# First loads of a fused attention and GEGLU block interleaved, a weight load cut by columns, and two of the first row norms moved to ScalarE

## The chip, the cores and the metric

The kernel runs on one core of one Trainium2 chip. The time is device time in microseconds (us) of one execution. TensorE is the matmul engine (PE in the profile), VectorE is DVE, ScalarE is ACT, GpSimd is POOL, SyncE is SP.

## The reference, cut to what matters

A transformer block with adaptive layer norm: linear attention, then a GEGLU feed-forward network. There are 2048 rows of 1024 columns in bf16, and the hidden width of the network is 3584.

```python
mod = (_silu(c) @ w_mod).reshape(c.shape[0], 6, 1, -1)
sa, ca, ga, sb, cb, gb = ...                        # six modulation rows of 1024
h = _layernorm(x, axis=-1) * (1 + ca) + sa
x = x + ga * _A_ref(h, A_wqkv, A_wo)                # linear attention
h = _layernorm(x, axis=-1) * (1 + cb) + sb
x = x + gb * (_gelu(h @ w_gate) * (h @ w_up) @ w_down)
```

At the start, the first products (V = h W_v) need the normed rows, the scale row `ca` and W_v; soon after, the shift row `sa` is needed.

Of the kernel before, what the change touches and what calls it, by code (L numbers as in the profile page):

```python
# [14 lines left out]
ALU = mybir.AluOpType  # L15
# [281 lines left out]
def kernel(  # L297
# [14 lines left out]
    P = 128  # L312
# [4 lines left out]
    S, D = x_in.shape  # L317
    F = B_w_gate.shape[1]
    KD = D // P
# [3 lines left out]
    TT = TG // P  # L323
# [38 lines left out]
    class Ring:  # L362


        def __init__(self, off, shape, dt, n):
            sz = 4 if dt == FP32 else 2
            for d in shape:
                sz *= d
            sz = max(sz, Plan.LINE)
            self.slots = [view(off + i * sz / KB, shape, dt) for i in range(n)]  # L370
            self.i = 0
# [188 lines left out]
    def load_w(dst, col, n=D, k0=0, k1=KD):  # L560
        sy.dma_start(out=dst, in_=A_wqkv[k0 * P:k1 * P, col:col + n].rearrange("(kd p) n -> p kd n", p=P))
# [41 lines left out]
    class ModRow:  # L603


        def __init__(self, m, wm, before={}):
            self.wm, self.ps, self.loads = wm, None, []
            for i in range(0, KD, 2):
                sy.dma_start(out=wm[:, i:i + 2, :],
                             in_=w_mod[i * P:(i + 2) * P, m * D:(m + 1) * D].rearrange("(k p) n -> p k n", p=P))  # L610
                self.loads.append(plan.ops[-1])
                if i in before:
                    plan.aim(before[i])

        def step(self, i):
            if i == 0:
# [39 lines left out]
        ac.activation(out=rstd, in_=rstd, func=AF.Exp, scale=-0.5)  # L656
        return rstd

    def ln_rows(xt):
        mv = ln_stats(xt)  # L660
        rstd = act_rstd(mv)
        xh = xh_ring()
        ve.tensor_scalar(out=xh, in0=xt, scalar1=mv[:, 0:1], scalar2=rstd[:, 0:1],
                                op0=ALU.subtract, op1=ALU.mult)
        return xh

    def keep_warm(n, cols):

        for _ in range(n):
            te.matmul(psD()[:, 0:cols], lhsT=ident, rhs=selb.rearrange("p a b -> p (a b)")[:, 0:cols],  # L670
                             start=True, stop=True, skip_group_check=True)
# [7 lines left out]
        ve.tensor_copy(out=hs0[:, 0:KH, tl * P:(tl + 1) * P], in_=src[0])  # L679
        ac.activation(out=hs0[:, KH:KD, tl * P:(tl + 1) * P], in_=src[1], func=AF.Copy)  # L680

    def scale_wv(n):
        for kd in range(KD):
            ve.tensor_scalar_mul(out=Wvs[:, kd, n * NW:(n + 1) * NW], in0=Wv[:, kd, n * NW:(n + 1) * NW],
                                 scalar1=opcA[:, kd:kd + 1])

    def v_plain(tl, n):

        ps = psV0()
        for k in range(KD):  # L690
            te.matmul(ps, lhsT=hs0[:, k, tl * P:(tl + 1) * P], rhs=Wvs[:, k, n * NW:(n + 1) * NW],
                      start=(k == 0), stop=(k == KD - 1), skip_group_check=True)
        ac.activation(out=vta[:, tl][:, 4 * n:4 * n + 4, 0:P], in_=ps.rearrange("p (g e) -> p g e", e=P), func=AF.Copy)

    def start_phase():

        xs, loads = [], []
        for tt in range(TT):
            xs.append(load_x(tt))
            loads.append(plan.ops[-1])  # L700
            if tt == 0:
                plan.aim(c_load)
        ca = ModRow(1, wm_ca, {0: loads[0], 2: loads[1], 4: loads[2], 6: loads[3]})
        load_w(Wv[:, 0:KH, 0:NW], 2 * D, NW, 0, KH)
        load_w(Wv[:, KH:KD, 0:NW], 2 * D, NW, KH, KD)
        load_w(Wv[:, :, NW:D], 2 * D + NW, NW)
        plan.chain.append(plan.ops[-1])
        sa = ModRow(0, wm_sa)
        plan.chain += sa.loads
        load_w(Wk[:, :, 0:NW], D, NW)  # L710
        ve.tensor_copy(out=identb[0:KD, :], in_=ident[0:KD, 0:KD])
        pcc = psM(BF16)[:, 0:KD]
        te.transpose(pcc, c8[0:KD, :], identb[0:KD, :])
        ve.tensor_copy(out=ccol, in_=pcc)
        ac.activation(out=esig, in_=ccol, func=AF.Exp, scale=-1.0)
        ve.tensor_scalar_add(out=esig, in0=esig, scalar1=1.0)
        ve.reciprocal(out=esig, in_=esig)
        tt_op(scol, ccol, esig, ALU.mult)
        ve.tensor_copy(out=srep, in_=scol[:, :, None].to_broadcast((P, KD, DH)))
        c_done = plan.ops[-1]  # L720
        halves = [[psT(F16).rearrange("p (k t) -> p k t", k=4) for _ in range(2)] for _ in range(2)]
        xh, done = [], []
        for i, x in enumerate(xs):
            n = len(plan.ops)
            xh.append(ln_rows(x))
            if i > 1:
                plan.pairs += [(done[i - 2], op) for op in plan.ops[n:] if op.eng == "DVE"]
            done.append(plan.ops[-1])
            if len(xh) == 1:
                plan.aim(c_done)  # L730
        for i in range(KH):
            if i < 3:
                start_tile(halves[i % 2], i, xh[i])
            if i == 0:
                keep_warm(1, NW)
            ca.step(i)
        ca.columns(opcA, 1.0, lambda: keep_warm(2, NW))
        scale_wv(0)
        for tl in range(TT):
            v_plain(tl, 0)  # L740
            if tl == 1:
                start_tile(halves[1], 3, xh[3])
        scale_wv(1)
        v_plain(0, 1)
        v_plain(1, 1)
        for i in range(KH):
            sa.step(i)
        sa.columns(modT[:, 0:KD], 0.0, lambda: v_plain(2, 1))
        v_plain(3, 1)
        for kd in range(KD):  # L750
            ve.tensor_scalar(out=hr1[0][:, kd, :], in0=hs0[:, kd, :], scalar1=opcA[:, kd:kd + 1],
                             scalar2=modT[:, kd:kd + 1], op0=ALU.mult, op1=ALU.add)
        return plan.ops[-1]
# [18 lines left out]
    def ln1_block(b):  # L772
        plan.ahead = 4000 if b > 1 else 14000
        for tl in range(TT):
            xt = load_x(b * TT + tl)
            if b == 1:
                plan.chain.insert((1, 2, 5, 7)[tl], plan.ops[-1])
            mv = ln_stats(xt)
            rstd = pool_rstd(mv)
            nb = nb_ring()  # L780
            gp.tensor_scalar(out=nb, in0=mv[:, 0:1], scalar1=rstd, scalar2=-1.0, op0=ALU.mult, op1=ALU.mult)
            xh = xh_ring()
            ac.activation(out=xh, in_=xt, func=AF.Identity, scale=rstd, bias=nb)
            gp.dma_start(out=xa_scr[b][tl * P:(tl + 1) * P, :], in_=xh)
        sy.dma_start_transpose(out=hr1[b], in_=xa_scr[b][:])
        if b == NG - 1:
            wd_moves(hr1[b][:, 0, 0:1], NPR)
        for kd in range(KD):
            ve.tensor_scalar(out=hr1[b][:, kd, :], in0=hr1[b][:, kd, :], scalar1=opcA[:, kd:kd + 1],  # L789
                             scalar2=modT[:, kd:kd + 1], op0=ALU.mult, op1=ALU.add)  # L790
        if b != 2:
            paced_moves(hr1[b][:, KD - 1, 0:1], sums_copy[0:1] if b == 1 else sums_add[0:1])
        plan.ahead = 14000
# [1026 lines left out]
```

## The kernel before: the parts that the change and the argument touch

The kernel computes its large products by a fast scheme of block sums and differences (the `A1x = A21 - A22` below are such differences), which is why VectorE has so much to do in it.

**A list scheduler orders the whole program.** The kernel's lines do not issue instructions. They record operations, and at the end a planner orders them. TensorE keeps the recorded order. For VectorE, ScalarE, GpSimd and SyncE the order comes out of 32 forward sweeps over a cost model; each is followed by a backward sweep that gives every operation a new due time, and the best forward sweep is kept.

```python
    def order(self):
        ...
        for op in self.ops:
            op.due = op.n
        for i in range(2 * self.ROUNDS):
            forward(i >= self.ROUNDS)        # sweep over the cost model; the best result is kept
            ...
            t = self.sweep(True, lambda o: (-o.due, -o.n))
            for op in self.ops:
                op.due = best[0] * (1 - op.done / max(t, best[0]))
                if old:
                    op.due += self.KEEP * (old[op.n] - op.due)
            for a, b in [*zip(self.chain, self.chain[1:]), *self.pairs]:
                b.due = max(a.due, b.due)
        return [self.ops[n] for _, n in best[1]]

    def issue(self):
        with self.tc.manual_schedule():
            for op in self.order():
                ...                           # issue op on its engine
```

`plan.chain` is a list of loads that are to be issued in its order.

**The start.** The order of the first loads is set by `aim` and `chain`; the row norms take their statistics on VectorE.

```python
    def ln_rows(xt):
        mv = ln_stats(xt)                     # 2 bn_stats and 1 bn_aggr on VectorE
        rstd = act_rstd(mv)                   # 2 small ScalarE operations
        xh = xh_ring()
        ve.tensor_scalar(out=xh, in0=xt, scalar1=mv[:, 0:1], scalar2=rstd[:, 0:1],
                                op0=ALU.subtract, op1=ALU.mult)
        return xh
    ...
        ca = ModRow(1, wm_ca, {0: loads[0], 2: loads[1], 4: loads[2], 6: loads[3]})
        load_w(Wv[:, 0:KH, 0:NW], 2 * D, NW, 0, KH)
        load_w(Wv[:, KH:KD, 0:NW], 2 * D, NW, KH, KD)
        load_w(Wv[:, :, NW:D], 2 * D + NW, NW)
        plan.chain.append(plan.ops[-1])
        sa = ModRow(0, wm_sa)
        plan.chain += sa.loads
```

## Time and profile before

| kernel before | |
|---|---|
| median of 3 runs | 749.21 us (748.36 to 750.71) |
| median of all 6 runs, those beside the changed kernel included | 748.91 us (747.80 to 750.71) |
| span of the profiled execution | 746.4 us |
| TensorE idle in it | 16.4 us, of which 9.7 before 28.5 us |
| waits of TensorE from 31 to 740 us | 2.2 us, in three groups of 1.2 (four waits, the longest 0.4), 0.5 and 0.5 |

A row of a timeline has the start in us, the length in us, the engine, the line of the kernel, the operation, output and input, and how many such operations the row holds. In square brackets stands how long the engine had been idle before it, and what ended that. `mem` is on-chip memory, `psum` the accumulators, and the names with `_dram` are inputs; `xhs` is the DRAM scratch that the late norm's stores write, and `ts` the one with the sums of w_down.

### The profile page before, as it was taken

Reading aid. Unit: us, or ns where it says so; the run is one execution under the profiler, and the core shown is the slowest. Engines: PE = TensorE matmul, PEld = TensorE weight load, DVE = VectorE, ACT = ScalarE, POOL = GpSimd, SP = SyncE. Lnnn points to the kernel's source line nnn. Section 1 sums busy time; section 2 is a strip of 40 time slices with the busy share of each in tenths; the row PEclk is TensorE's granted clock in tenths of the full one; section 3 lists DMA queues with packets and bytes.
Section 4 is the critical chain, followed back from the end, with each engine's and each line's share of the span. In section 5 each row is a group of like instructions: output and inputs, shape, how many; then the busy total and the mean of one; then the engine's idle time right before and its main releaser. Section 6 shows DMA issues by size and latency. Waiting matters only on the chain.

```text
span 746.4 us, 11439 instructions
## 1 busy us (share of the span) xinstructions
PE 730.0 (98%) x4164; PEld 388.7 (52%) x4164; DVE 589.5 (79%) x1258; ACT 433.0 (58%) x757; POOL 95.8 (13%) x164
## 2 busy tenths in 40 slices
PE   5999999999999999999999999999999999999997
PEld 2444445444444455545454586545555555548664
DVE  6897997577786878777997888678888888888763
ACT  3665576669752768997876234027777777731000
POOL 2331245000001113342311000010000000000000
PEclk9999999999999999999999999999999999999999
DMA  8974479828899979899659799654131322399822
GB/s 298 322 212 132 152 182 163 299 101 258 245 290 257 364 253 261 259 318 227 187 191 237 210 281 314 206 183 132 60 114 57 112 73 98 110 276 302 278 104 71
DMA packets 151832, 152.79 MB, mean 205 GB/s; under 512 B 33824, under 2 KB 128544, under 8 KB 150496
## 3 DMA queue, kind: packets, MB, share of 16 engines
q1 hardware_dynamic: 128832, 122.44, 53.7%
q0 software_dynamic: 20592, 27.53, 15.6%
q10 hardware_dynamic: 2352, 2.10, 0.8%
q8 instruction: 32, 0.52, 0.3%
q14 instruction: 24, 0.20, 0.1%
HBM read 123.34 MB, written 36.04 MB: 214 GB/s over the span
## 4 chain that ended last, share of the span: by engine, by line
PE 84%; DVE 6%; ACT 5%; DMA 3%; issue 1%; SPq 1%; ACTq 0%; DVEq 0%
PE psum L1382 30%; PE psum L1588 13%; PE psum L1632 9%; PE psum L870 8%; PE psum L1393 7%; PE psum L1262 7%; PE psum L940 5%; DVE mem L564 5%; PE psum L969 4%; DMA mem<-in_A_wqkv_dram 2%; DMA mem<-in_w_mod_dram 1%; PE psum L984 1%; ACT mem L815 1%; DVE psum L564 1%; ACT psum L1436 1%
## 5 line engine op out<-in xcount | busy, mean ns | idle before, releaser
L564 DVE TENSOR_TENSOR mem<-mem 128x512 f16<-128x512 f16 (+8 forms) x669 | 307.8, 507 | 23.1 <-ACT mem L815 10.1
L1382 PE MATMUL psum<-mem 128*128 128x512 f16 x1248 | 299.1, 379 | 0.8 <-ACT psum L1436 0.5
L815 ACT ACTIVATE mem<-psum 128x256 f32<-128x256 f32 (+3 forms) x284 | 154.3, 562 | 119.9 <-PE psum L1382 45.1
L564 DVE TENSOR_TENSOR mem<-psum,mem 128x512 f16<-128x512 f32 (+4 forms) x204 | 155.4, 767 | 72.8 <-ACT mem L815 29.5
L1382 PEld LDWEIGHTS <-mem 128*128 128x128 f16 (+1 forms) x1248 | 122.0, 98 | 112.1 <-issue 2.7
L1588 PE MATMUL psum<-mem 128*128 128x512 f16 (+2 forms) x462 | 99.2, 373 | 0.5 <-DVE mem L564 0.5
L1393 PE MATMUL psum<-mem 128*128 128x256 f16 x560 | 89.5, 272 | 1.3 <-DVE psum L564 1.2
L1393 PEld LDWEIGHTS <-mem 128*128 128x128 f16 (+1 forms) x560 | 54.7, 98 | 46.8 <-issue 5.1
L1588 PEld LDWEIGHTS <-mem 128*128 128x128 f16 x462 | 45.2, 98 | 49.8 <-issue 0.7
L1632 PE MATMUL psum<-mem 128*128 128x256 f16 (+1 forms) x588 | 66.2, 273 | 0.0
L870 PE MATMUL psum<-mem 128*128 128x512 f16 (+1 forms) x280 | 62.9, 379 | 0.0
L1632 PEld LDWEIGHTS <-mem 128*128 128x128 f16 x588 | 57.5, 98 | 9.2
L1436 ACT ACTIVATE psum<-psum 128x512 f32<-128x512 f32 x56 | 32.8, 587 | 41.3 <-PE psum L1382 28.9
L1262 PE MATMUL psum<-mem 128*128 128x512 f16 x256 | 56.0, 379 | 0.0
L940 PE MATMUL psum<-mem 128*128 128x512 f16 x224 | 51.2, 379 | 0.0
L564 DVE TENSOR_TENSOR psum<-psum,mem 128x256 f32<-128x256 f32 x80 | 34.3, 429 | 17.7 <-ACT mem L815 17.3
L870 PEld LDWEIGHTS <-mem 128*128 128x128 f16 x280 | 26.9, 97 | 31.8 <-DVE mem L789 1.2
L1262 PEld LDWEIGHTS <-mem 128*128 128x128 bf16 x256 | 24.8, 98 | 30.3 <-issue 0.8
L1453 ACT ACTIVATE mem<-psum 128x512 f16<-128x512 f32 x56 | 33.1, 595 | 10.9 <-PE psum L1382 10.5
L1463 ACT ACTIVATE mem<-mem 128x512 f16<-128x512 f16 x56 | 34.9, 625 | 1.5 <-DVE mem L564 1.1
L940 PEld LDWEIGHTS <-mem 128*128 128x128 f16 (+1 forms) x224 | 21.5, 98 | 27.0 <-issue 2.0
L1049 POOL DMA_DIRECT2D ts<-in_B_w_down_dram x28 | 28.3, 1199 | 9.2 <-DMA ts<-in_B_w_down_dram 8.9
(132 smaller groups left out, 525.3 us busy)
## 6 DMA issues: line engine op xcount, KB each, us to landing
mem<-in_B_w_gate_dram SPq DMA_DIRECT2D x14, 1024.0 KB, 7.0
mem<-in_B_w_up_dram SPq DMA_DIRECT2D x14, 1024.0 KB, 5.4
mem<-in_w_mod_dram SPq DMA_DIRECT2D x24, 512.0 KB, 5.9
mem<-ts SPq DMA_DIRECT2D x6, 1792.0 KB, 6.8
mem<-in_A_x_dram SPq DMA_DIRECT2D x32, 256.0 KB, 7.7
ts<-in_B_w_down_dram POOLq DMA_DIRECT2D x28, 256.0 KB, 6.3
mem<-ub SPq DMA_DIRECT2D x16, 448.0 KB, 6.7
mem<-in_B_w_down_dram SPq DMA_DIRECT2D x12, 448.0 KB, 7.8
```

The costliest lines, as they stand in the source:

```text
L564: ve.tensor_tensor(out=out, in0=a, in1=b, op=op)
L815: ac.activation(out=t, in_=ps, func=AF.Copy)
L870: te.matmul(ps, lhsT=A[:, k, i * P:(i + 1) * P], rhs=B[:, k, :], start=(start and k == 0), stop=(k == KH - 1), skip_group_check=True)
L940: te.matmul(o, lhsT=W[:, k, (j0 + i) * P:(j0 + i + 1) * P], rhs=h_form(a, k), start=(start and k == 0), stop=(k == KH - 1), skip_group_che ...
L1262: te.matmul(psw[:, half, :], lhsT=pqT[b][:, g, tl * P:(tl + 1) * P], rhs=Wp[:, g, half * NW:(half + 1) * NW], start=(g == 0), stop=(g == K ...
L1382: te.matmul(ps, lhsT=a[:, k, e, :], rhs=b[:, k, :], start=(start and k == 0), stop=(k == KH - 1), skip_group_check=True)
L1393: te.matmul(ps, lhsT=self.x[a][:, k, :], rhs=self.y[y][:, k, :], start=(start and k == 0), stop=(k == KH // 2 - 1), skip_group_check=True)
L1436: ac.activation(out=z, in_=x, func=AF.Copy)
L1453: ac.activation(out=o, in_=ps, func=AF.Gelu_apprx_tanh)
L1463: ac.activation(out=o, in_=o, func=AF.Gelu_apprx_tanh)
L1588: te.matmul(psm[:, q, c], lhsT=A[:, i, q * P:(q + 1) * P], rhs=wt[:, i, c], start=(start and i == 0), stop=(i == NPR - 1), skip_group_chec ...
L1632: te.matmul(ps[:, q, :], lhsT=a[:, k, q * P:(q + 1) * P], rhs=y[:, k, :], start=(start and q == 0 and k == 0), stop=(k == NPR // 2 - 1), s ...
```

## The change

The intent is to start TensorE's real work sooner. The scale row's quarters are loaded between the first row tiles, so that it is complete earlier. The first half of W_v comes as two quarters by columns, so that its first 256 columns can be scaled and multiplied before the rest is there. The statistics of row tiles 2 and 3 go from VectorE to ScalarE. The recorded order of the start follows. The diff, cut to its core:

```diff
-    def ln_rows(xt):
+    def ln_rows(xt, by_act):
+        xh = xh_ring()
+        if by_act:
+            nmean, rstd = act_stats(xt)
+            ve.tensor_scalar(out=xh, in0=xt, scalar1=nmean, scalar2=rstd[:, 0:1], op0=ALU.add, op1=ALU.mult)
+            return xh
         mv = ln_stats(xt)
...
-    def scale_wv(n):
+    def scale_wv(c):
         for kd in range(KD):
-            ve.tensor_scalar_mul(out=Wvs[:, kd, n * NW:(n + 1) * NW], in0=Wv[:, kd, n * NW:(n + 1) * NW],
-                                 scalar1=opcA[:, kd:kd + 1])
+            ve.tensor_scalar_mul(out=Wvs[:, kd, c], in0=Wv[:, kd, c], scalar1=opcA[:, kd:kd + 1])
...
+    START_LOADS = "c a0 x0 a1 x1 a2 a3 v0 x2 v1 x3 v2".split()
...
-        ca = ModRow(1, wm_ca, {0: loads[0], 2: loads[1], 4: loads[2], 6: loads[3]})
-        load_w(Wv[:, 0:KH, 0:NW], 2 * D, NW, 0, KH)
-        load_w(Wv[:, KH:KD, 0:NW], 2 * D, NW, KH, KD)
-        load_w(Wv[:, :, NW:D], 2 * D + NW, NW)
-        plan.chain.append(plan.ops[-1])
+        ca = ModRow(1, wm_ca)
+        loads.update((f"a{i}", op) for i, op in enumerate(ca.loads))
+        for name, c in (("v0", slice(0, HB)), ("v1", slice(HB, NW)), ("v2", slice(NW, D))):
+            load_w(Wv[:, :, c], 2 * D + c.start, c.stop - c.start)
+            loads[name] = plan.ops[-1]
+        plan.chain += [loads[name] for name in START_LOADS]
...
-            xh.append(ln_rows(x))
+            xh.append(ln_rows(x, i in (2,3,)))
...
-        scale_wv(0)
-        for tl in range(TT):
-            v_plain(tl, 0)
-            if tl == 1:
-                start_tile(halves[1], 3, xh[3])
-        scale_wv(1)
+        scale_wv(slice(0, HB))
+        for tl in range(2):
+            v_plain(tl, 0, slice(0, HB))
+        scale_wv(slice(HB, NW))
+        start_tile(halves[0], 2, xh[2])
+        for tl in range(2):
+            v_plain(tl, 0, slice(HB, NW))
+        v_plain(2, 0)
+        start_tile(halves[1], 3, xh[3])
+        v_plain(3, 0)
+        scale_wv(slice(NW, D))
```

More of the change, by code (lines that the diff above doesn't have):

```diff
@@ L603, with __init__ @@
     class ModRow:
-        def __init__(self, m, wm, before={}):
+        def __init__(self, m, wm):
             self.wm, self.ps, self.loads = wm, None, []
@@ L611, in __init__ @@
                 self.loads.append(plan.ops[-1])
-                if i in before:
-                    plan.aim(before[i])
         def step(self, i):
@@ L657, in act_rstd @@
         return rstd
-    def ln_rows(xt):
+    def ln_rows(xt, by_act):
[4 more added lines that the diff above has]
+            return xh
         mv = ln_stats(xt)
         rstd = act_rstd(mv)
-        xh = xh_ring()
         ve.tensor_scalar(out=xh, in0=xt, scalar1=mv[:, 0:1], scalar2=rstd[:, 0:1],
@@ L680, in start_tile, with v_plain, v_out @@
         ac.activation(out=hs0[:, KH:KD, tl * P:(tl + 1) * P], in_=src[1], func=AF.Copy)
-    def scale_wv(n):
+    def scale_wv(c):
         for kd in range(KD):
-            ve.tensor_scalar_mul(out=Wvs[:, kd, n * NW:(n + 1) * NW], in0=Wv[:, kd, n * NW:(n + 1) * NW],
-                                 scalar1=opcA[:, kd:kd + 1])
-    def v_plain(tl, n):
-        ps = psV0()
-        for k in range(KD):
-            te.matmul(ps, lhsT=hs0[:, k, tl * P:(tl + 1) * P], rhs=Wvs[:, k, n * NW:(n + 1) * NW],
-                      start=(k == 0), stop=(k == KD - 1), skip_group_check=True)
+            ve.tensor_scalar_mul(out=Wvs[:, kd, c], in0=Wv[:, kd, c], scalar1=opcA[:, kd:kd + 1])
+    v_banks = {}
+    def v_plain(tl, n, c=slice(0, NW)):
+        if c.start == 0:
+            v_banks[tl, n] = psV0()
+        ps = v_banks[tl, n]
+        for k in range(KD):
+            te.matmul(ps[:, c], lhsT=hs0[:, k, tl * P:(tl + 1) * P], rhs=Wvs[:, k, n * NW + c.start:n * NW + c.stop],
+                      start=(k == 0 and c.start == 0), stop=(k == KD - 1), skip_group_check=True)
+        if c.stop == NW:
+            v_out(tl, n, ps)
+    def v_out(tl, n, ps):
         ac.activation(out=vta[:, tl][:, 4 * n:4 * n + 4, 0:P], in_=ps.rearrange("p (g e) -> p g e", e=P), func=AF.Copy)
+    START_LOADS = "c a0 x0 a1 x1 a2 a3 v0 x2 v1 x3 v2".split()
     def start_phase():
-        xs, loads = [], []
+        xs, loads = [], {"c": c_load}
         for tt in range(TT):
             xs.append(load_x(tt))
-            loads.append(plan.ops[-1])
-            if tt == 0:
-                plan.aim(c_load)
-        ca = ModRow(1, wm_ca, {0: loads[0], 2: loads[1], 4: loads[2], 6: loads[3]})
-        load_w(Wv[:, 0:KH, 0:NW], 2 * D, NW, 0, KH)
-        load_w(Wv[:, KH:KD, 0:NW], 2 * D, NW, KH, KD)
-        load_w(Wv[:, :, NW:D], 2 * D + NW, NW)
-        plan.chain.append(plan.ops[-1])
+            loads[f"x{tt}"] = plan.ops[-1]
+        ca = ModRow(1, wm_ca)
[4 more added lines that the diff above has]
+        plan.chain += [loads[name] for name in START_LOADS]
         sa = ModRow(0, wm_sa)
@@ L730, in start_phase @@
                 plan.aim(c_done)
-        for i in range(KH):
-            if i < 3:
-                start_tile(halves[i % 2], i, xh[i])
-            if i == 0:
-                keep_warm(1, NW)
+        keep_warm(1, NW)
+        ca.step(0)
+        start_tile(halves[0], 0, xh[0])
+        for i in range(1, KH):
             ca.step(i)
+        start_tile(halves[1], 1, xh[1])
         ca.columns(opcA, 1.0, lambda: keep_warm(2, NW))
-        scale_wv(0)
-        for tl in range(TT):
-            v_plain(tl, 0)
-            if tl == 1:
-                start_tile(halves[1], 3, xh[3])
-        scale_wv(1)
+        scale_wv(slice(0, HB))
[9 more added lines that the diff above has]
+        scale_wv(slice(NW, D))
         v_plain(0, 1)
@@ L776, in ln1_block @@
             if b == 1:
-                plan.chain.insert((1, 2, 5, 7)[tl], plan.ops[-1])
+                plan.chain.insert(len(START_LOADS) + (0, 1, 4, 6)[tl], plan.ops[-1])
             mv = ln_stats(xt)
```

## The prediction

> **What bounds the kernel now.** I read the page first, then a table of engine busy time by stretch, then the chain of work that ended last over the first 60 us, then TensorE's and SyncE's rows in time order there, then the DMA view for three stretches. The page's first block:
>
> ```profile
> span 746.4 us, 11439 instructions
> PE 730.0 (98%) x4164; PEld 388.7 (52%) x4164; DVE 589.5 (79%) x1258; ACT 433.0 (58%) x757; POOL 95.8 (13%) x164
> ```
>
> TensorE is busy 98%: the whole program holds 16.4 us in which it is not. The change touches the first 30 us only, so what it could ever win is what lies idle there. By stretch (columns: stretch, length, busy us of PE, PEld, DVE, ACT, POOL with counts, granted clock, DMA share, GB/s):
>
> ```profile
> 0.00:8.00 8.00, 0.30 (x3) 0.23 (x4) 5.40 (x28) 2.49 (x6) 3.79 (x22) 1.00 0.68 208
> 8.00:15.00 7.00, 5.88 (x47) 3.02 (x47) 5.48 (x15) 2.56 (x7) 0.00 (x0) 1.00 1.05 370
> 15.00:28.50 13.50, 12.61 (x73) 5.56 (x73) 9.85 (x28) 6.50 (x10) 3.49 (x10) 1.00 1.07 371
> 28.50:40.00 11.50, 11.50 (x69) 5.00 (x69) 10.24 (x25) 7.04 (x11) 3.51 (x7) 1.00 0.78 244
> ```
>
> TensorE idles 7.7 us before 8 us, 1.1 us to 15, 0.9 us to 28.5, and nothing after. The DMA share is 1.05 and more from 8 to 28.5: the queue is full. So before 28.5 us the loads, not TensorE, set the pace. The chain that ended last says which load (start us, us, what):
>
> ```profile
> 7.39 11.51 DMA mem<-in_A_wqkv_dram
> 18.90 0.02 issue
> 18.92 9.11 DMA mem<-in_w_mod_dram
> 28.02 0.04 issue
> 28.07 0.40 PE psum L636 x4
> 28.46 1.83 PE psum L691 x8
> ```
>
> Line 636 is the product of the modulation row. The load issued at 18.92 is the last quarter of the shift row (sa), which lands at 28.02; TensorE takes it at 28.07 and is never idle for long again. TensorE's own rows say the same:
>
> ```profile
> 7.88 1.03 PE L676 MATMUL psum<-mem 128*128 128x128 f16 x8 [5.53 <-DVE mem L663]
> 15.03 4.18 PE L691 MATMUL psum<-mem 128*128 128x512 f16 x16 [0.66 <-DVE mem L684]
> 26.50 0.83 PE L636 MATMUL psum<-mem 128*32 128x512 bf16 x12
> 28.07 0.40 PE L636 MATMUL psum<-mem 128*32 128x512 bf16 x4 [0.73 <-DMA mem<-in_w_mod_dram]
> ```
>
> The reader should see that TensorE reached the shift row at 26.50, did three quarters of it, and waited for the fourth. Anything gained earlier than this ends in that wait, as long as the order there is kept.
>
> **What the Trainium skill says.** "DMA: Bandwidth & Descriptors", section Specifications, gives at least 512 B as the transfer for line rate. The trace disagrees with reading that as "512 B is as good as 2 KB". In three stretches with a full queue, first with rows of 1 KB (W_v), then 2 KB (x and w_mod), then 512 B (quarters of the down weights):
>
> ```profile
> 13.00:17.50 4.50, 3.45 (x19) 1.19 (x19) 3.50 (x11) 0.39 (x3) 0.00 (x0) 1.00 1.10 349
> 20.00:25.00 5.00, 5.00 (x25) 2.28 (x24) 5.00 (x14) 1.65 (x4) 1.41 (x5) 1.00 1.05 387
> 683.00:687.00 4.00, 4.00 (x39) 3.59 (x37) 3.93 (x8) 0.60 (x1) 0.00 (x0) 1.00 1.18 290
> ```
>
> 349, 387 and 290 GB/s. The measurement decides: shorter rows are slower here.
>
> The same page, "Anatomy of one DMA", puts the fixed part of a DMA at about 2.0 us, mostly the wait until the last byte is confirmed. The trace agrees roughly: the first x tile is issued at 1.22 and VectorE's first statistics start at 3.89, 2.67 us, of which 0.262 MB at 387 GB/s is 0.68.
>
> "ScalarE: Activation LUTs", Rules for kernel authors, gives about 0.3 us per ACTIVATE plus 0.83 ns per element, 1.15 us for 1024. The trace has 1.23 us for such a pass (line 783, 128x1024). I use 1.23. "TensorE: Matmul & The Clock Gate", Part 1, says the array runs at half rate until some 3.4 us of sustained work. The trace agrees in kind: eight transposes took 1.03 us at 7.88 and 0.61 us at 19.05.
>
> **The change part by part.**
>
> Order of loads. Before: c, four x tiles (1.05 MB), four quarters of the scale row ca (2.10), W_v in 0.52, 0.52 and 1.05. After: c, x0, ca0, x1, ca1 to ca3, x2, two W_v column quarters (0.52 each), x3, the W_v half (1.05). What follows is unchanged: x4, x5, sa0, sa1, x6, sa2, x7, sa3, then W_k. The bytes ahead of sa3's end are the same 8.39 MB. The order as built confirms this. So in bytes nothing moves at the point that binds.
>
> Row length. The two W_v loads were 512 columns of half the rows (1 KB runs) and are now 256 columns of all rows (512 B runs). 1.05 MB at 349 GB/s is 3.00 us, at 290 it is 3.62. So +0.6 us in the queue, on the path: sa3 lands that much later.
>
> Ramp. The DMA rate is 208 GB/s over the first 8 us; a table by half microseconds has a share of 0.48 and 148 GB/s from 4.5 to 5.0, with four small x loads at the head of the queue. Putting a 0.5 MB load second may keep the engines fuller. I estimate the loss of this dip, against a full queue, at about 1 us, and that the new order recovers a third of it: -0.3 us. This is a guess about a cause that I have not seen.
>
> Norm on ScalarE. For tiles 2 and 3 VectorE loses four statistics of 677 ns and two aggregates of 201 ns, 3.1 us. ScalarE gains two passes of 1.23 us for each, 4.9 us in all, between about 12 and 19 us, where it was busy less than half of the time. x2 now lands near 12.2 us, so its norm is ready near 15.2; x3 near 16.3, ready near 19.2. Off the binding path if TensorE still reaches sa3 in time.
>
> Scaling W_v. Eight operations of 512 columns in 2.43 us (0.30 each) become 16 of 256; from 0.30 at 512 and 0.53 at 1024 columns I estimate 0.2 each, so 3.2 us: +0.8 us of VectorE. It pays for itself by starting after one quarter.
>
> TensorE. 16 products of 512 columns become 32 of 256, equal in columns. My walk, load by load: x0 lands at 3.9, ca0 near 6, x1 near 7. VectorE as built does x1's statistics before it normalises x0, so the first transposes come near 9.0, against 7.88. ca3 lands near 11.6 against 12.9, so the scale columns are ready near 13.7 against 14.6. The first W_v quarter lands near 13.9; products start near 14.2 against 15.0 and are paced by VectorE until about 18; tile 2 ends near 20.8; the half of W_v lands near 19.4 and tile 3's norm waits with it, so tile 3 ends near 23.8; two more groups of eight at 0.217 us bring TensorE to the shift row at 27.2, against 26.50, and through three quarters of it at 28.1. Then sa3: 28.0 + 0.6 - 0.3 = 28.3. The two nearly meet. TensorE passes this point near 28.4 against 28.07.
>
> After it: the same 718.3 us of TensorE work (746.4 - 28.07). The built order of TensorE is the same from there; VectorE and ScalarE have some dozens of neighbours swapped, worth 0.3 us either way by the 2.7 us of waits TensorE has in the rest. Sum: +0.3 us on the span. On 749.2 that is 749.5; I take 0.2 off because such an order is likely to have been kept for a gain. Predicted 749.3 us.
>
> **The rivals.**
>
> 1. The start really shortens. For: the scale row is complete 1.3 us sooner and products start 0.8 us sooner. Against: TensorE's order around sa3 is unchanged and bytes before it are the same. If the ramp recovers its whole 1 us, sa3 lands at 28.0 + 0.6 - 1.0 = 27.6; TensorE, at 28.1, then binds: no change. If it also runs ahead of my walk: -0.7, 748.5 us.
>
> 2. TensorE becomes late. For: tile 3 hangs on a chain x3, four ScalarE steps, VectorE, transposes, two copies, in a queue behind scalings; and its sparser early work may leave the array at half rate longer (transposes and fills cost some 0.9 us more). Against: 32 paced products give it time to speed up. It would pass sa3 near 29.2: +1.1, 750.3 us.
>
> 3. The quarters' short rows cost more, as the slowest of 16 DMA queues decides a landing (sa3's bytes were through by about 26 by the sum of the rates, it landed at 28.0): +1.2, 750.4 us.
>
> **Range and chances.** Before itself ran from 748.36 to 750.71, so a median of few runs moves by some 0.6. The rivals span -0.7 to +1.2. Together: 747.8 to 750.9 for 8 in 10. 2% is 15 us, as much as all idle time of TensorE; faster or slower by that has 1% each, within 2% has 98%.
>
> **What would show it.** Right: the chain of waits again runs through the modulation load into line 634 (the same product), at 28.0 to 28.9 us; TensorE waits there for DMA or arrives with it; DMA near 290 GB/s while the W_v quarters load. Wrong: sa3 landing before 27.5 us (ramp), or TensorE arriving after it with waits on VectorE or ScalarE in front of tile 3 (rival 2), or a difference that arises after 30 us, where I expect none over 0.5.

## More of the kernel before

In the middle of the program, gate and up products of the first half of the rows end, and the down product begins.

**The middle.** Three parts of the program meet near 390 to 405 us. First, the norm of late row tiles writes each normed tile to DRAM; GpSimd issues the store:

```python
        def tile_norm(tl):                    # in late_norm
            xt, xh = x2e_ring(), xhe_ring()
            ...
            ac.activation(out=xh, in_=xt, func=AF.Identity, scale=rstd, bias=nb)
            gp.dma_start(out=xh_scr[g][b % 2][r:r + P, :], in_=xh)      # "the store", L1226
```

Second, GpSimd also issues the moves that make sums of blocks of w_down, from DRAM to DRAM, 256 KB each, half of them accumulating:

```python
    def move(dst, src, add):                  # "the moves", L1049
        gp.dma_start(out=dst, in_=src, **(dict(accum_op=ALU.add) if add else {}))
```

Third, before the down product VectorE makes the differences of blocks of the hidden layer, in chunks:

```python
        for c in range(NPR // NC):            # in down_out
            cs = slice(c * NC, (c + 1) * NC)
            ve.tensor_tensor(out=A1x[:, cs, :], in0=A21[:, cs, :], in1=A22[:, cs, :], op=ALU.subtract)   # L1566
            ve.tensor_tensor(out=A21[:, cs, :], in0=A11[:, cs, :], in1=A21[:, cs, :], op=ALU.subtract)
```

The first and the third share memory. Offsets are in KB of a partition:

```python
    A11, A12, A21, A22, A1x = (at(88 + 14 * i, [NPR, TG], F16) for i in range(5))   # A1x: 144 to 158
    xhe_ring = Ring(150, [D], F16, 3)                                               # 150 to 156
```

So a chunk of A1x in the space of a normed tile may only be written once the store of that tile has read it, that is, once it has landed. Chunks elsewhere need not wait for it.

## The result, and the profile after

| | before | after |
|---|---|---|
| median of 6 runs each | 748.91 us (747.80 to 750.71) | 752.84 us (751.12 to 754.59) |
| ratio, after over before | | 1.0053 (95%: 1.0033 to 1.0073) |
| span of the profiled execution | 746.4 us | 751.1 us |

A ratio here and below is the mean time of the one kernel's runs over that of the other's of the same rounds, so not quite the ratio of the two medians. The change is 2% neither way; but the kernel is slower by half a per cent, and 752.84 us lies outside the predicted range of 747.8 to 750.9.

The page of the changed kernel, first block:

```profile
span 751.1 us, 11472 instructions
...
PE 731.8 (97%) x4166; PEld 391.6 (52%) x4180; DVE 588.4 (78%) x1260; ACT 438.0 (58%) x765; POOL 97.4 (13%) x164
```

TensorE is busy 1.8 us more (731.8 against 730.0), and idle 19.3 us instead of 16.4.

**The start went much as predicted, but for the wait at the shift row.** The table by stretch for the changed kernel, with the columns that the prediction lists, and TensorE's rows in time order:

```profile
0.00:8.00 8.00, 1.39 (x6) 0.31 (x6) 4.68 (x26) 2.18 (x5) 3.80 (x22) 1.00 0.74 252
11.50:14.50 3.00, 2.42 (x16) 1.44 (x15) 2.10 (x11) 2.89 (x7) 0.00 (x0) 1.00 1.17 304
```

```profile
8.25 1.03 PE L678 MATMUL psum<-mem 128*128 128x128 f16 x8 [2.01 <-DVE mem L665]
...
13.41 3.56 PE L696 MATMUL psum<-mem 128*128 128x256 f16 x16 [0.58 <-DVE mem L686]
...
26.92 1.13 PE L634 MATMUL psum<-mem 128*32 128x512 bf16 x16
```

The DMA queue moved 252 GB/s in the first 8 us, against 208. While the W_v quarters came in it moved 304. The first transposes start at 8.25 us, the first products at 13.41, and TensorE is at the shift row at 26.92, where all sixteen products now run in one go: there is no wait for a load in this row. It ends this row at 28.05, where the kernel before ended it at 28.47. That is one profile of each; the profiles of the experiments show below how much this point scatters.

**The loss is in the middle.** TensorE's order after the start is the same in both kernels, so the same products can be laid side by side. Before, then after, from the rows of TensorE:

```profile
400.46 0.60 PE L1393 MATMUL psum<-mem 128*128 128x256 f16 x4
...
402.63 0.38 PE L1393 MATMUL psum<-mem 128*128 128x256 f16 x2
...
405.65 0.38 PE L1393 MATMUL psum<-mem 128*128 128x256 f16 x2
```

```profile
399.62 0.60 PE L1409 MATMUL psum<-mem 128*128 128x256 f16 x4
...
405.54 0.38 PE L1409 MATMUL psum<-mem 128*128 128x256 f16 x2 [3.60 <-DVE psum L564]
...
410.25 0.38 PE L1409 MATMUL psum<-mem 128*128 128x256 f16 x2
```

The reader should pair the lines. The first pair differs by -0.84 us: at 400 us the changed kernel still leads. The second differs by +2.91, after a wait of 3.60 us for a VectorE sum. The third differs by +4.60. From there on the lag stays between 4.6 and 4.7 us to the last row of products (it starts at 741.28 us before, at 745.99 after). So the wait takes 3.75 us and the five microseconds after it 1.7 us more, and nothing else in the 350 us that follow matters.

Why did VectorE come late? Its rows, before and after:

```profile
398.93 0.68 DVE L1566 TENSOR_TENSOR mem<-mem 128x1024 f16<-128x1024 f16 x1
...
400.36 0.69 DVE L1566 TENSOR_TENSOR mem<-mem 128x1024 f16<-128x1024 f16 x1
...
401.57 0.42 DVE L564 TENSOR_TENSOR psum<-psum,mem 128x256 f32<-128x256 f32 x1
```

```profile
403.25 0.69 DVE L1582 TENSOR_TENSOR mem<-mem 128x1024 f16<-128x1024 f16 x1 [4.14 <-DMA xhs<-mem]
...
404.46 0.68 DVE L1582 TENSOR_TENSOR mem<-mem 128x1024 f16<-128x1024 f16 x1
405.06 0.43 DVE L564 TENSOR_TENSOR psum<-psum,mem 128x256 f32<-128x256 f32 x1
```

Before, two chunks of the A1x difference (L1566) run at 398.93 and 400.36 and the sum for TensorE at 401.57. After, the first of the two chunks (L1582, the same line moved by the change) waited 4.14 us for the landing of the store `xhs<-mem`, and the sum for TensorE, which stands behind it in VectorE's order, ran at 405.06. The chain of work that ended last in the changed kernel says it in one piece (start, length, what):

```profile
393.20 10.03 DMA xhs<-mem
...
405.15 0.35 DVE psum L564
...
405.54 0.38 PE psum L1409 x2
```

The store was issued at 393.20 and took 10.03 us to land. Then GpSimd's rows, before and after, tell why:

```profile
391.65 1.26 POOL L1049 DMA_DIRECT2D ts<-in_B_w_down_dram  x1
393.25 0.59 POOL L1226 DMA_DIRECT2D xhs<-mem  x1 [0.33 <-ACT mem L815]
393.81 1.22 POOL L1049 DMA_DIRECT2D ts<-in_B_w_down_dram  x1
```

```profile
391.55 2.42 POOL L1065 DMA_DIRECT2D ts<-in_B_w_down_dram  x2
393.20 1.36 POOL L1242 DMA_DIRECT2D xhs<-mem  x1
```

Before, the store (L1226) stands between the last two moves of w_down. After, both moves (L1065 x2) stand ahead of it: the row starts at 391.55 and ends at 393.97, and the store's own begins inside it. The tile view of the same store in the kernel before:

```profile
DMA to landing us min/median/max: 7.1/7.1/7.1
```

It took 7.1 us there. Issued at 393.25, it landed at 400.35, and the chunk that had to wait for it started at 400.36. That is a transfer landing at the very moment when it is needed, with no wait in the profile to show that it had no slack.

The order as built shows a second exchange, this one on VectorE: of the two A1x chunks, the kernel before has the one that waits for nothing first (398.93), and the one in the space of the store's tile second (400.36). The changed kernel has them the other way round. So the chunk that must wait is asked for one place sooner, while its store lands later.

The last 1.7 us are a clock. The table by single microseconds of the changed kernel (the third column from the right is the granted clock):

```profile
406.00:407.00 1.00, 1.00 (x4) 0.45 (x3) 1.00 (x3) 0.58 (x1) 0.00 (x0) 0.50 0.10 16
...
408.00:409.00 1.00, 1.00 (x4) 0.32 (x3) 0.65 (x2) 0.87 (x2) 0.00 (x0) 0.50 1.06 361
409.00:410.00 1.00, 1.00 (x5) 0.43 (x4) 0.00 (x0) 0.00 (x0) 0.00 (x0) 0.82 1.09 383
```

From about 406 to 409 us TensorE worked at half its clock. In the kernel before, the clock is 1.00 from 405 to 410. In the changed kernel the products slow down with it: four products of L1398 took 1.03 us at 398.75 and 1.72 at 405.76. The Trainium skill, "TensorE: Matmul & The Clock Gate", Part 1, says that the array falls to half rate after an idle window of about 3.4 us and comes back after about as long of sustained work. The trace agrees: 3.60 us idle, then a little over 3 us at 0.50; half of 3.3 us is the 1.7 us lost.

### The profile page after: what moved, and what is told of

Same layout as the page of the kernel before. It is cut to its first block, busy times and chain, and to the rows that moved or that the text cites. A ratio compares the mean times of both kernels' runs of the same rounds, so it can differ in the third digit from the quotient of the medians.

```text
span 751.1 us, 11472 instructions
## 1 busy us (share of the span) xinstructions
PE 731.8 (97%) x4166; PEld 391.6 (52%) x4180; DVE 588.4 (78%) x1260; ACT 438.0 (58%) x765; POOL 97.4 (13%) x164
## 4 chain that ended last, share of the span: by engine, by line
PE 83%; DVE 7%; ACT 4%; DMA 3%; issue 2%; SPq 0%; POOL 0%; ACTq 0%; DVEq 0%
PE psum L1398 29%; PE psum L1604 13%; PE psum L1648 9%; PE psum L886 8%; PE psum L1409 6%; DVE mem L564 6%; PE psum L956 5%; PE psum L1278 5%; PE psum L985 4%; PE psum L696 2%; DMA xhs<-mem 1%; PE psum L1000 1%; DMA mem<-in_w_mod_dram 1%; ACT mem L831 1%; DVE psum L564 1%
## 5 line engine op out<-in xcount | busy, mean ns | idle before, releaser
L1398 PE MATMUL psum<-mem 128*128 128x512 f16 x1248 | 300.4, 380 | 0.7 <-ACT psum L1452 0.5
L1398 PEld LDWEIGHTS <-mem 128*128 128x128 f16 (+1 forms) x1248 | 122.3, 98 | 112.8 <-issue 3.7
L1065 POOL DMA_DIRECT2D ts<-in_B_w_down_dram x28 | 28.2, 1210 | 9.4 <-DMA ts<-in_B_w_down_dram 9.2
```

The costliest lines, as they stand in the source:

```text
L1398: te.matmul(ps, lhsT=a[:, k, e, :], rhs=b[:, k, :], start=(start and k == 0), stop=(k == KH - 1), skip_group_check=True)
```

## The experiments

The theory after reading the traces: the start costs and gains nothing that can be measured; the loss comes from two exchanged pairs of neighbours near 393 and 400 us, which the scheduler made because the start had changed. Its rivals: the start itself is slower (shorter rows in the queue, or a late norm), or the lower granted clock of the changed kernel (0.995 to 0.999 in its runs, 1.000 in most of those before) is the cause and not a consequence, or the many other exchanged neighbours add up. Kernels that are told together ran in the same job on the same chip. All kernels gave correct results.

### One pair in each direction, and the start and the rest apart

The first two kernels move one GpSimd operation. On the changed kernel, the store goes ahead of the last move (3217 is the store's place counted from the end of the recorded program):

```diff
-            for op in self.order():
+            order = self.order()
+            store = next(i for i, op in enumerate(order) if op.n == len(order) - 3217)
+            move = max(i for i in range(store) if order[i].eng == "POOL")
+            order.insert(store, order.pop(move))
+            for op in order:
```

> The changed kernel with one pair of GpSimd's DMA issues exchanged back: the last store of a normalised tile goes ahead of the second accumulating move of the down weights, as it stood in the kernel before. Theory Q (the store queued behind the move lands 3 us later, VectorE waits for it, TensorE stalls 3.6 us and loses its clock): the wait of VectorE for this store and the stall near 402 us go, the granted clock is 1.000, and the time falls by 5 us, to 747.5 to 748.5 us, below the kernel before by its gain at the start. Rival S (the shifted start makes loads and work collide later, whatever that pair's order): within 1.5 us of the changed kernel, 751.5 to 754. Rival C (the lower clock is the cause, not the consequence): clock again below 1.000, time above 751.

On the kernel before, the reverse: the next move goes ahead of the store.

```diff
+            move = min(i for i in range(store + 1, len(order)) if order[i].eng == "POOL")
```

> The kernel before with the same pair exchanged the other way, nothing else: the store is issued behind the second move. Theory Q: VectorE waits 3 to 4 us for the store near 400 us, TensorE stalls 2.5 to 3.5 us, clock below 1.000, time 752 to 754 us (before: 748.9). Rivals S and C: no change from the kernel before, 748 to 750 us.

The other two take the recorded start of one kernel and the order of the other's rest. Of the last 6293 operations recorded, the 2269 on VectorE, ScalarE, GpSimd and SyncE are put into the other kernel's order, which is embedded as a list; dependences are kept.

```diff
-            for op in self.order():
+            for op in pinned(self.order()):    # the rest in the other kernel's order
```

> The changed start phase, with every operation recorded after it kept in the order of the kernel before on VectorE, ScalarE, GpSimd and SyncE. Theory Q: as e1 or a little better, 747.5 to 748.5 us, the shift row passed near 27.6 us, no stall near 402. Rival S: 751.5 to 754 us, since the start is the changed one.

> The start phase of the kernel before, with everything after it in the order of the changed kernel. Theory Q: the stall near 402 us is there although nothing of the change's text is, 752.5 to 755 us. Rival S: 748 to 750 us, as the kernel before.

| kernel | median us (range, runs) | ratio to before (95%) | landing of the store | VectorE's wait for it |
|---|---|---|---|---|
| before, same job | 748.86 (747.68 to 750.40, 11) | 1 | 7.1 us (in its own profile) | 0 |
| e1, changed, store ahead of the move | 749.87 (747.77 to 751.80, 6) | 1.0021 (1.0006 to 1.0036) | 7.1 | 1.24 |
| e2, before, store behind the move | 750.10 (749.98 to 751.21, 5) | 1.0022 (1.0010 to 1.0034) | 9.1 | 2.17 |
| e3, new start, old rest | 748.96 (748.71 to 750.32, 5) | 1.0005 (0.9993 to 1.0017) | 6.6 | 0 |
| e4, old start, new rest | 751.96 (750.14 to 753.25, 6) | 1.0042 (1.0028 to 1.0056) | 9.4 | 3.54 |

The start and the rest come apart cleanly. With the old rest the new start costs 0.05%, and the interval holds zero. With the new rest, even the old start, not a line of which was changed, is 0.42% slower. So the loss is in the order of the rest. In e4 TensorE stood idle for 2.98 us in front of the same sum:

```profile
404.29 0.58 PE L1393 MATMUL psum<-mem 128*128 128x256 f16 x2 [2.98 <-DVE psum L564]
```

The clock was 1.00 up to this wait and 0.50 in the two full microseconds after 405: the slow clock follows the stall, also where the start is the old one.

The exchange on GpSimd alone carries about half of the loss, in both directions. e1 missed its 747.5 to 748.5 us, and e2 its 752 to 754 us, its stall of 2.5 to 3.5 us (1.3 measured) and its lowered clock (1.00). e3 and e4 came out some 0.5 us outside their expected ranges, and far from those of the rival. And e1 is still about 1 us above before, and its VectorE row shows why:

```profile
399.84 0.69 DVE L1586 TENSOR_TENSOR mem<-mem 128x1024 f16<-128x1024 f16 x1 [1.24 <-DMA xhs<-mem]
```

The store lands as early as before, 7.1 us after its issue, and yet a chunk waits 1.24 us for it. It is asked for sooner. This left the exchange on VectorE to be tried.

### Both pairs, and what remains

On the changed kernel, e5 makes e1's exchange and also swaps the two A1x chunks back; e6 swaps the chunks alone.

```diff
+            i, j = (next(i for i, op in enumerate(order) if op.n == len(order) - key) for key in (2932, 2930))
+            order[i], order[j] = order[j], order[i]
```

> The changed kernel with two pairs exchanged back: GpSimd's last store ahead of the second move (as in e1), and on VectorE the difference chunk that has to wait for that store put behind the next chunk, which waits for nothing. Theory Q2 (the loss at 402 us is the product of both exchanges: the store lands later, and the waiting chunk is asked for earlier): no wait of VectorE for that store over 0.5 us, clock 1.000, time 748.0 to 749.3 us, 0.5 to 1.5 us below e1 (749.87). Rival (the rest of e1's 1 us over the kernel before is something else, spread over the many other exchanges): e5 equals e1, 749.5 to 750.5.

> The changed kernel with VectorE's pair of chunks exchanged back only; the store stays behind the move. Theory Q2: the store still lands near 403 us, VectorE waits for it about 1.2 us less than in the changed kernel because one chunk is done meanwhile, so 751.0 to 752.3 us, between the changed kernel (752.8) and e1. Rival (VectorE's order has no part): 752.5 to 753.5.

The trace of the changed kernel has a second wait that the kernel before does not have: near 210 us VectorE waited 4.2 us for another `xhs` store, this one in SyncE's queue, and TensorE 1.47 us. e7 is e5 with, in addition, SyncE's order of the rest as in the kernel before, which takes that wait away.

> e5, and SyncE's issues after the start in the order of the kernel before. The changed kernel's other stall is near 210 us, where a store of a normalised tile is issued behind loads of the denominators and VectorE waits 4.2 us for it. Theory Q2 with that second wait: no stall over 0.5 us near 210, time 0.5 to 1 us below e5, 747.3 to 748.5 us, and this would be the fastest of all. Rival: the gain before 194 us is lost elsewhere, time as e5.

e8 is e3 with the first half of W_v loaded by halves of its rows, in runs of 1 KB, as in the kernel before, and not by columns:

```diff
-        for name, c in (("v0", slice(0, HB)), ("v1", slice(HB, NW)), ("v2", slice(NW, D))):
-            load_w(Wv[:, :, c], 2 * D + c.start, c.stop - c.start)
+        for name, c, k in (("v0", slice(0, NW), (0, KH)), ("v1", slice(0, NW), (KH, KD)), ("v2", slice(NW, D), (0, KD))):
+            load_w(Wv[:, k[0]:k[1], c], 2 * D + c.start, c.stop - c.start, *k)
```

> e3 (changed start, the rest as before), with the first half of W_v loaded in halves of the rows with 1 KB runs again, in place of quarters of the columns with 512 B runs. If short rows cost 0.6 us of the load queue, the DMA rate over that half is near 350 GB/s in place of 290, and the last W_v load lands 0.5 to 0.7 us earlier after the ramp. As the first products now wait for both halves, they start 0.8 us later; time 748.3 to 749.8 us, the same as e3 within its noise. If short rows cost nothing, the rate is equal.

| kernel | median us (range, runs) | ratio to before (95%) | landing of the store | VectorE's wait for it |
|---|---|---|---|---|
| before, same job | 748.87 (747.90 to 750.44, 11) | 1 | | |
| e5, changed, both pairs back | 748.05 (747.39 to 748.73, 5) | 0.9989 (0.9977 to 1.0002) | 7.8 us | 0.76 |
| e6, changed, VectorE's pair back | 750.84 (749.45 to 751.62, 6) | 1.0024 (1.0011 to 1.0037) | 9.4 | 2.29 |
| e7, e5 without the wait at 210 us | 748.48 (748.11 to 749.04, 5) | 0.9995 (0.9983 to 1.0007) | 7.2 | 0 |
| e8, e3 with 1 KB rows | 748.96 (747.40 to 750.21, 4) | 0.9994 (0.9977 to 1.0011) | 6.9 | 0 |

VectorE's rows of e5 and then of e6 at the chunk that waits:

```profile
401.32 0.69 DVE L1588 TENSOR_TENSOR mem<-mem 128x1024 f16<-128x1024 f16 x1 [0.76 <-DMA xhs<-mem]
```

```profile
402.68 0.69 DVE L1585 TENSOR_TENSOR mem<-mem 128x1024 f16<-128x1024 f16 x1 [2.29 <-DMA xhs<-mem]
```

With e1 the four corners are complete, all on the changed kernel, though measured in three jobs (each had its own runs of the kernel before, with medians of 748.86 to 748.91 us): neither pair back 752.84 us, the store alone 749.87 (-2.97), the chunks alone 750.84 (-2.00), both 748.05 (-4.79). The two nearly add, and which of them is larger is not shown, since the intervals of e1 and e6 overlap. Both of them back leaves nothing of the loss, so the dozens of other exchanged neighbours are together worth nothing that can be seen here; some win and some lose, as the wait at 210 us below shows. The rival of a sum of many small things falls. In the details e5 and e6 missed a little: VectorE still waited 0.76 us in e5, where at most 0.5 was expected, and e6 is just below its 751.0 us. The clock falls as a first cause too: in e5 and e6, with the longest wait of TensorE for this sum at 0.3 and 1.7 us, the granted clock from 405 to 410 us was 1.00. The row of e6:

```profile
405.00:410.00 5.00, 4.99 (x26) 2.28 (x24) 2.14 (x5) 3.70 (x7) 0.00 (x0) 1.00 1.00 323
```

The profile of e6 is that of its fastest execution (749.45 us), as is that of e1; their slower ones were not seen.

e7 gave nothing beyond e5 (748.48 against 748.05 us, intervals that overlap), and TensorE's rows say where the gain went:

```profile
186.11 1.02 PE L962 MATMUL psum<-mem 128*128 128x512 f16 x4 [1.47 <-DVE mem L570]
```

The wait at 210 us is gone, and one of 1.47 us stands at 186 instead. Under it, VectorE waits 2.01 us for a `den` load, a buffer of the attention's denominators, which SyncE issues in another place now. One wait was turned into another of the same size, so this run does not say what the wait at 210 us is worth. In the changed kernel it ate a lead: matched products have it 1.6 us ahead of the kernel before at 194 us, level after the wait (210.59 against 210.62) and still at 333 us (332.80 against 332.85), and 0.85 ahead at 387 us (386.43 against 387.28). So this wait is not what puts the changed kernel behind, and e5, which has a wait of 1.5 us there too, is level with the kernel before.

e8 shows that the short rows cost rate, and no time that these runs can resolve. The table by stretch, e3 and then e8:

```profile
11.50:13.50 2.00, 2.00 (x18) 1.28 (x15) 1.02 (x2) 1.64 (x3) 0.00 (x0) 1.00 1.19 304
```

```profile
11.50:13.50 2.00, 2.00 (x18) 1.36 (x15) 1.02 (x2) 1.80 (x3) 0.00 (x0) 1.00 1.10 365
```

304 against 365 GB/s in the same two microseconds, with the same median of 748.96 us. The 0.6 us that the prediction put on the short rows is 0.08%, and the interval of e8 is 0.17% wide to each side, so the medians alone could not show it; TensorE's rows at the shift row, below, say more.

### The two parts of the start, and another queue for the store

e9 is e3 without the norm on ScalarE; e10 is the kernel before with that norm alone, the old loads, and its own order of the rest.

```diff
-            xh.append(ln_rows(x, i in (2,3,)))
+            xh.append(ln_rows(x, False))
```

> e3 (changed start, the rest as before) without the norm on ScalarE: tiles 2 and 3 take their statistics on VectorE as in the kernel before. If the norm on ScalarE matters at the start, TensorE passes the shift row later than in e3 (28.5 us) by up to the 1.5 us that VectorE then works more before the scalings, and the time is 749.5 to 750.5. My theory, that the load of the shift row and not the engines sets that point: within 0.6 us of e3, 748.5 to 749.6.

```diff
-            xh.append(ln_rows(x))
+            xh.append(ln_rows(x, i in (2, 3)))
```

> The kernel before with the norm of tiles 2 and 3 on ScalarE alone, its loads and everything after the start as before. The shift row's load binds, so no gain: TensorE passes it at 27.3 to 28.5 us and waits for the load, time 748.3 to 749.5 us.

e11 leaves the changed kernel's order as it is and issues the one store from ScalarE; e12 also has the two chunks swapped back.

```diff
+            q = next(op for op in order if op.n == len(order) - 3217)
+            q.eng = "ACT"
```

> The changed kernel in its own order, but the one late store is issued by ScalarE, right after it has made the tile, in place of GpSimd. Theory Q2 says that the store lands late because it stands behind the accumulating move in GpSimd's own DMA queue. On another queue it lands 3 to 7 us after its issue in place of 10, VectorE waits under 1 us, clock 1.000, time 748.0 to 749.3 us. Rival (it lands late because the DMA engines are loaded there, whichever queue it is in): it lands 9 us or more after its issue and the time is 751 to 753.

> e11 with VectorE's pair of chunks exchanged back too. Theory Q2: the wait for the store is gone entirely, time as e5 or slightly below, 747.5 to 748.5 us. If e11 already has no wait, the same as e11 within 0.5 us.

| kernel | median us (range, runs) | ratio to before (95%) |
|---|---|---|
| before, same job | 748.94 (748.23 to 750.66, 9) | 1 |
| e9, e3 without the ScalarE norm | 750.31 (749.85 to 750.66, 4) | 1.0022 (1.0007 to 1.0037) |
| e10, before with the ScalarE norm | 749.21 (748.48 to 749.47, 4) | 1.0004 (0.9990 to 1.0018) |
| e11, store in ScalarE's queue | 750.01 (749.02 to 750.03, 5) | 1.0012 (1.0000 to 1.0025) |
| e12, e11 and VectorE's pair back | 748.54 (747.46 to 749.23, 5) | 0.9996 (0.9983 to 1.0008) |

TensorE's rows at the shift row, e9 and then e10:

```profile
28.94 1.05 PE L634 MATMUL psum<-mem 128*32 128x512 bf16 x16
```

```profile
28.07 0.40 PE L636 MATMUL psum<-mem 128*32 128x512 bf16 x4 [1.09 <-DMA mem<-in_w_mod_dram]
```

e9 went against the theory and came out in the range of the rival. Without the norm on ScalarE, TensorE comes to the shift row at 28.94 us (27.88 in e3), and finds all of it there. How strong is this? Eight profiles have the loads and the norm of the changed kernel (after, e1, e3, e5, e6, e7, e11, e12). In them TensorE comes to the shift row at 26.33 to 28.55 us, and the two that came early did wait for its last quarter, as the prediction had it. These are the rows of e5:

```profile
26.33 0.83 PE L640 MATMUL psum<-mem 128*32 128x512 bf16 x12
27.92 0.40 PE L640 MATMUL psum<-mem 128*32 128x512 bf16 x4 [0.76 <-DMA mem<-in_w_mod_dram]
```

In e6 it waited 0.44 us, until 28.11. So with the new loads either TensorE or the load can end last; which of them does differs from profile to profile. e9 is later than all eight, in the one profile there is. By the ratios the norm on ScalarE is worth about 1.3 us there (1.0022 against 1.0005 of two jobs), but the two intervals overlap, so the size is not settled. In e10, with the old loads, TensorE arrives early and waits 1.09 us for the last quarter, which it gets at 28.07, the very time of the kernel before: the load binds, and the norm is worth nothing. So neither part of the start gains anything alone, and together they end level.

e11 lies in the middle, in neither of the two ranges that were expected. Issued by ScalarE at 394.52 us, later than GpSimd would have, the store landed about 7.6 us later at 402.1, and VectorE waited 1.85 us. The Trainium skill, "DMA: Bandwidth & Descriptors", section "Queues, rings and completion order", says that every queue row has a ring of its own on each DMA engine. This trace agrees that far: out of the ring with the two moves ahead of it, the same store lands in 7.6 us and not in 10.0. Of the 2.8 us between e11 and the changed kernel, this run cannot say how much is the ring, since the time of issue changed as well. e12, with the chunk asked for later, is level with the kernel before; VectorE still waited 1.04 us for the store there, where no wait was expected. It is a second way to the same end, by moving the store and not the order.

No version was shown to beat the kernel before. e5 is the fastest, 748.05 us, but its interval reaches 1.0002.

## Why the prediction was wrong, by its own steps

- **The bound.** Right: TensorE sets the time, and what is lost shows up as its idle time. Of the 3.9 us between the medians nearly all is one wait and its clock.
- **The rate with short rows.** Right: 290 GB/s predicted, 304 measured over 11.5 to 14.5 us, against 365 with 1 KB rows (e8). The +0.6 us that it was to cost was "on the path" in the prediction. In the profiles of e3 and e8 it is not: TensorE does all of the shift row in one go, at 27.88 and 28.26 us. In e5 and e6 the load of that row does end last, so there it can count.
- **The ramp.** The guess of -0.3 us has about the right size. The old order (before, e2, e4, e10) moved 208 to 239 GB/s in the first 8 us, mean 220; the new one (ten profiles) 228 to 252, mean 240. 20 GB/s over 8 us are 0.16 MB, or 0.4 us at 387 GB/s. The ranges overlap, and the cause of the scatter was not seen.
- **The walk through the start.** First transposes 9.0 predicted, 8.25 measured; first products 14.2 and 13.41; at the shift row 27.2 and 26.92, in the profile of the changed kernel. Right so far.
- **The wait at the shift row.** "Then sa3: 28.0 + 0.6 - 0.3 = 28.3" did not hold in that profile: nothing is waited for after 26.92, and the chain that ended last runs through the last quarter of the scale row (landed at 10.27 us) and then through TensorE and VectorE, not through the shift row's load. In e5 and e6 the load does end last, at 27.92 and 28.11. TensorE left the row at 28.05 to 29.60 us in the eight profiles (median 28.7) and at 27.67 to 28.47 in the three with the old start (before, e2, e4; median 28.2), so some 0.5 us later, where +0.3 was predicted. Part of the scatter fits the half rate that rival 2 names: the first sixteen products took 2.51 us in e5 and e6 and 3.56 or 3.57 in the other six. The column of the granted clock reads 1.00 in these early stretches in all of them, so it does not confirm this. And e3, which has all of the start and nothing else, is at 1.0005 (-0.5 to +1.3 us). The end of this part is right within the noise; the wait that was to set it is found in two profiles of eight.
- **Rivals 1 and 2.** Both describe some of the profiles: in six of eight TensorE, and not the load, ends last at the shift row. In the changed kernel's own profile the row is passed 0.42 us sooner than before (rival 1), in e1, e3, e7, e11 and e12 later than before (rival 2). Rival 3, a still later landing of the shift row, is not seen: in e5 and e6 it landed by 28.11, and in the changed kernel's own profile before the row ended at 28.05.
- **After the start.** This step failed, in the words "After it: the same 718.3 us of TensorE work" and "VectorE and ScalarE have some dozens of neighbours swapped, worth 0.3 us either way by the 2.7 us of waits TensorE has in the rest". What it named as showing it wrong came true: a difference that arises after 30 us, where it expected none over 0.5. The rest took 3 to 5 us more: e4 has it with the old start (751.96 against 748.86), and e5 removes it by two pairs (748.05 against 752.84). The error is in how the term was sized. The 2.7 us of waits that TensorE has in the profile before bound what a better order could gain. They say nothing of what a worse order could lose: that depends on the slack of the transfers, and not on the waits seen. The row at 400.36 us, a chunk that started the moment its store had landed, had no slack at all, and the prediction did not look for such rows. It also counted the exchanges on VectorE and ScalarE and passed over GpSimd, where one store behind one more move was about half of the loss.

How 4.6 us of lag come about, in one sum from the rows: a lead of 0.85 us, then 3.75 us of stall, then about 1.7 us by half clock: -0.85 + 3.75 + 1.7 = 4.6.

What stays open: what the wait at 210 us is worth; why the store takes about 7 us even with one move ahead of it, when the fastest of the eight such stores in the kernel before took 2.4 us; why e1's executions scatter over 4 us; and why the scheduler's sweeps end in this order, which was read from its code as a consequence of changed due times, but not traced sweep by sweep.

## What to carry to other kernels

Where a scheduler orders the whole program, an edit at one end is an edit everywhere: compare the built order of every engine, the DMA-issuing ones too, and for each exchanged pair ask which transfer it delays or which consumer it hastens. Existing waits bound the gain of a reordering, while what it can lose depends on the slack of the transfers, so look for operations that start within some tenths of a microsecond of a landing. And test a change of the start with the order of the rest held fixed, or its own worth of 0.05% is read as 0.5%.

## What the Trainium skill lacked or had wrong

- "DMA: Bandwidth & Descriptors", Specifications, puts line rate at 512 B and more. Here runs of 512 B gave 304 GB/s (e3) where runs of 1 KB gave 365 (e8) in the same stretch of the same program.
- The same page, "Anatomy of one DMA", gives the fixed part of a single DMA; no page gives what a DMA costs behind others in GpSimd's ring. A 256 KB store landed 6.6 to 7.8 us after its issue with one 256 KB move just ahead of it (before, e1, e3, e5), and 9.1 to 10.0 with two (after, e2, e4, e6).
- "TensorE: Matmul & The Clock Gate", Part 1, names an idle window of about 3.4 us. Here 2.98 us of idle time were followed by a clock of 0.50 as well (e4); 1.7 us were not (e6).
- No page has the rate of the DMA queue at the start of a kernel: 208 to 252 GB/s over the first 8 us in the profiles here, against 371 from 15 to 28.5 us in both kernels.
- "DMA: Bandwidth & Descriptors", Specifications, gives about 358 GB/s as a core's limit from HBM; the row lacks the condition, which the page states further down, that both cores of a pair stream at once. Here one core ran alone, and from 20 to 25 us of the kernel before, with loads of x and w_mod in the queue, 387 GB/s were moved.
